# Pooled attention and a gated channel mix on one core: the product with v in groups of 128, 128, 128, 128 and 64 queries

## The chip, the cores and the metric

The kernel runs on one core of a Trainium2 chip. Such a core has five engines that run side by side, each through its own list of instructions in a fixed order: TensorE (PE, matrix products; PEld is its loading of weights), VectorE (DVE), ScalarE (ACT), GpSimd (POOL) and SyncE (SP, which here issues all DMAs). They wait for each other through semaphores. The metric is the time on the device in microseconds (us), the median of the timed runs.

## The reference

Inputs are q, k and v of 8 images x 8 heads x 1152 positions x 64, and the weights of the channel mix. What is computed, cut to what matters:

```python
q_pool = q.reshape(B, H, S // 2, 2, D).mean(axis=3)          # 576 queries for each head
scores = (1 / sqrt(D)) * q_pool @ k.transpose(0, 1, 3, 2)    # 576 x 1152
attn = exp(scores - scores.max(-1))
attn = attn / (attn.sum(-1) + 1e-9)
x = (attn @ v), heads side by side                           # 8 x 576 x 512
x_prev = x moved by one position, zeros first
xk = mu_k * x + (1 - mu_k) * x_prev                          # xr the same with mu_r
k = relu(xk @ w_k) ** 2                                      # 576 x 1024
out = sigmoid(xr @ w_r) * (k @ w_v)                          # 576 x 512
```

All inputs are float32. The kernel keeps their precision with pairs of 16-bit numbers: each operand is a high part and a low part, and a product is three products (high by high, high by low, low by high).

## The kernel before

**Attention.** The 64 pairs of image and head (heads, from here on) follow each other. A head's 576 queries are 6 blocks of 96, its 1152 keys 9 chunks of 128. For each block, PE multiplies the 9 chunks of keys with the block's queries into one of three PSUM tiles `s` (L473), DVE takes the maximum over the chunks (L480), PE turns it (L483), DVE takes it over the keys (L486), PE brings it back (L488), ACT writes the bound into a spare row of the queries' low part (L491), PE adds the remaining products (L497), and ACT takes the exponential (L503). The exponentials go as 32-bit numbers into `pf`, whose last axis is the 576 queries of a head. The upper 16 bits of each are read in place as a 16-bit number: the high part. POOL turns the lower 16 bits into a tile of their own, `pl` (L505): the low part.

**The product with v.** It is made by `window`. Its groups are 128 queries wide, since the exponentials are the weights that PE loads and PE takes 128 columns. 576 is four and a half times 128, and before the change five groups start at queries 0, 128, 256, 352 and 448 (`WIN`), so that groups 3, 4 and 5 overlap by 32 queries each time. For every group PE does, for each of the 9 chunks, two products with the high part (with v's high part and a column of ones, 65 wide, L523; with v's low part, 64 wide, L525) and one with the low part (65 wide, L530): 27 products, 135 for a head. All five groups add up side by side in one PSUM tile, `a`, which is there once. When the last group is done, DVE adds a guard to the sums (L545), inverts them (L547) and multiplies (L548) into `xb`. After every second head PE turns `xb` through the same tile `a` (L560), and ACT copies it into `xt`, in two pieces of 384 and 192 queries (L563).

**The channel mix.** Its rows are taken 256 at a time over the images. ACT and DVE make xk and xr (L632, L635), ACT and POOL their parts (L641, L643), and PE makes the three products (all on L663) into PSUM tile `f`. Rows of an image can be mixed when the last two heads of this image are in `xt`. The float32 weights are turned into pairs during the first heads: 20 pieces, each with one DMA, three steps on DVE (L594, L595, L597), two on ACT (L592, L599) and one on POOL (L600).

**What sets the order.** The kernel doesn't issue an operation where it is written. `op` records each piece with its engine, an assumed duration, the names that it reads and writes, and a key (a due time); `Issue.run` then plays the whole program with these durations and an assumed delay between engines, tries some orders, and writes the best one out. So each engine's list is fixed when the program is built, and one changed operation can move others everywhere. A group's key is that of the block after which it can begin (`after` in the last lines of the loop over heads).

Of the kernel before, what the change touches and what calls it, by code (L numbers as in the profile page):

```python
# [29 lines left out]
SQ = 0.25  # L30
# [3 lines left out]
SHIFT = 18.0  # L34
LO, VLO = 2.0 ** -28, 2.0 ** -12
# [223 lines left out]
def kernel(  # L259
# [20 lines left out]
    QN = 96  # L280
# [1 line left out]
    T = 256  # L282

    WIN = [(0, 1), (128, 2), (256, 3), (352, 4), (448, 5)]
    NW = len(WIN)
    TURN = [(0, 3, 0), (3, 5, 384)]
    assert D == 64 and DM == NG * P and TQ == NB * QN == WIN[-1][0] + P

    const = ctx.enter_context(tc.tile_pool(name="const", bufs=1))  # L290
    psum = ctx.enter_context(tc.tile_pool(name="psum", bufs=1, space=PSUM))
# [13 lines left out]
    def half(x, dt, t):  # L305

        return x.bitcast(dt).rearrange("p c (q t) -> p c q t", t=2)[:, :, :, t]
# [18 lines left out]
    NV = 3  # L326
    vt = bufs("vt", NV, [P, NC, 2 * D + 2], F16)
    vb = bufs("vb", NV, [P, NC, D + 2], F16)
    pf = const.tile([P, NC, TQ], I32, name="pf")
    pl = const.tile([P, NC, TQ], F16, name="pl")  # L330
    mx, mb = bufs("mx", 3, [P, QN], F16), bufs("mb", 3, [P, 1], F16)
    den, xb = bufs("den", 2, [P, NW], F32), bufs("xb", 1, [P, NW, 2, D], F32)
# [120 lines left out]
    def block(n, j, i, t):  # L453

        hp, z = n % 2, i % 3
        qi = n // 2 % 2
        q0 = hp * TQ + j * QN
        qhi, qlo = (qT[qi][:, r].rearrange("p j x -> p (j x)")[:, q0:q0 + QN] for r in (0, 1))
        kh, kl = ([(t_, qi, hp, j, j0) for j0, j1 in ((0, 5), (5, NQ)) if q0 < j1 * P and q0 + QN > j0 * P]
                  for t_ in ("qT", "qTl"))  # L460
        s = s_b[z]
        rows = slice(j * QN, (j + 1) * QN)
        mxz, mbz = mx[z], mb[z]

        def cols(c0, c1):
            return s[:, P + c0 * QN:P + c1 * QN]

        def grid(c0, c1):
            return cols(c0, c1).rearrange("p (c q) -> p c q", q=QN)

        def scores(c0, c1):
            for c in range(c0, c1):
                nc.tensor.matmul(cols(c, c + 1), ks1[hp][:, c, :], qhi,  # L473
                                 start=(c == c0), stop=False, skip_group_check=True)
# [5 lines left out]
        op("DVE", 0.967, lambda: nc.vector.tensor_reduce(mxz, grid(0, NC).rearrange("p c q -> p q c"),  # L480
                                                         axis=AX.X, op=ALU.max),
           r=[("s", z)], w=[("mx", z)], key=t)
        op("PE", 0.054, lambda: nc.tensor.matmul(s[0:QN, 0:P], mxz, identb, start=False, stop=False,  # L483
                                                 skip_group_check=True),
           r=[("mx", z)], w=[("s", z)], key=t + O_MAX)
        op("DVE", 0.199, lambda: nc.vector.tensor_reduce(mbz[0:QN], s[0:QN, 0:P], axis=AX.X, op=ALU.max),  # L486
           r=[("s", z)], w=[("mb", z)], key=t + O_MAX)
        op("PE", 0.05, lambda: nc.tensor.matmul(s[:, 0:QN], mbz[0:QN].broadcast_to([QN, P]),  # L488
                                                 negi[0:QN, 0:QN], start=False, stop=False, skip_group_check=True),
           r=[("mb", z)], w=[("s", z)], key=t + O_MAX)  # L490
# [12 lines left out]
        op("ACT", NC * QN / 1200 + 0.051, lambda: nc.scalar.activation(  # L503
            pf[:, :, rows], grid(0, NC), AF.Exp, bias=SHIFT, scale=0.125 / (2.0 * SQ)), r=[("s", z)], w=[("pf", j)], key=t + O_EXP)
        op("POOL", NC * QN / 1000 + 0.066, lambda: nc.gpsimd.tensor_scalar(  # L505
            pl[:, :, rows], half(pf, U16, 0)[:, :, rows], LO, 1.0, op0=ALU.mult, op1=ALU.mult),
           r=[("pf", j)], w=[("pl", j)], key=t + O_REST)

    def window(n, w, t):

        b, h = divmod(n, H)
        g, hh = divmod(h, 2)
        r0 = WIN[w][0]
        jv = n % NV
        VN = D + 1
        vk = [(x, jv, c0) for x in ("vt", "vtl") for c0 in (0, 5)]
        js = range(r0 // QN, (r0 + P - 1) // QN + 1)
        a0, rows = w * VN, slice(r0, r0 + P)

        def hi(c0, c1):
            for c in range(c0, c1):
                nc.tensor.matmul(a_b[:, a0:a0 + VN], half(pf, F16, 1)[:, c, rows], vt[jv][:, c, D:D + VN],  # L523
                                 start=(w == 0 and c == 0), stop=False, skip_group_check=True)
                nc.tensor.matmul(a_b[:, a0:a0 + D], half(pf, F16, 1)[:, c, rows], vt[jv][:, c, 0:D],  # L525
                                 start=False, stop=False, skip_group_check=True)

        def lo(c0, c1):
            for c in range(c0, c1):
                nc.tensor.matmul(a_b[:, a0:a0 + VN], pl[:, c, rows], vb[jv][:, c, 0:VN],  # L530
                                 start=False, stop=(c == NC - 1), skip_group_check=True)

        for c0 in (0, 3, 6):
            op("PE", 3 * 0.0595, lambda c0=c0: hi(c0, c0 + 3),
               r=vk + [("pf", j) for j in js] + ([("a",)] if c0 or w else []), w=[("a",)], key=t)
# [9 lines left out]
        op("DVE", 0.075, lambda: nc.vector.tensor_scalar(dz, u[:, :, D], GUARD, None, op0=ALU.add),  # L545
           r=[("a",)], w=[("den", z)], key=t + O_EVAC)
        op("DVE", 0.08, lambda: nc.vector.reciprocal(dz, dz), r=[("den", z)], w=[("den", z)], key=t + O_EVAC)  # L547
        op("DVE", 0.07 + NW * D / 960, lambda: nc.vector.tensor_tensor(  # L548
            xz[:, :, hh], u[:, :, 0:D], dz.unsqueeze(2).broadcast_to([P, NW, D]), op=ALU.mult),
           r=[("den", z), ("a",)], w=[("xb", hh)], key=t + O_EVAC)  # L550
        if hh == 0:
            return
        for k0, k1, q0 in TURN:
            base = WIN[k0][0]
            qe = WIN[k1 - 1][0] + P

            def turned(k0=k0, k1=k1, base=base):
                for k_ in range(k0, k1):
                    r_ = WIN[k_][0] - base
                    nc.tensor.transpose(a_b[:, r_:r_ + P], xz[:, k_].rearrange("p h d -> p (h d)"), ident)  # L560

            op("PE", 0.11 * (k1 - k0), turned, r=[("xb", 0), ("xb", 1)], w=[("a",)], key=t + O_TURN)
            op("ACT", 0.051 + (qe - q0) / 1200, lambda q0=q0, qe=qe, base=base: nc.scalar.copy(  # L563
                xt[b % 3][:, g, 1 + q0:1 + qe], a_b[:, q0 - base:qe - base]),
               r=[("a",)], w=[("xt", b % 3, g, k0)], key=t + O_TURN)
# [52 lines left out]
    def mix(w, t0, t1, key, dk):  # L618
# [4 lines left out]
        for c in range(NG):  # L623
            t = t0
            while t < t1:
# [4 lines left out]
                xk = [("xt", b % 3, c, k0) for k0, k1, q0 in TURN  # L630
                      if q0 < s0 + ln and WIN[k1 - 1][0] + P > s0 - 1]
# [112 lines left out]
    for n in range(B * H):  # L744
# [5 lines left out]
        for j in range(NB):  # L750
            i = n * NB + j
            block(n, j, i, i * PER)
            for w, (_, after) in enumerate(WIN):
                if after == j:
                    window(n, w, i * PER + O_AV)
        if h == H - 1:
# [42 lines left out]
```

## Time and profile before

| | us |
|---|---|
| median of three runs | 1169.64 |
| the three runs | 1169.64, 1169.77, 1166.29 |
| span of the profiled execution, first to last instruction | 1166.8 |
| PE busy | 1116.0 (96%) |
| PE's weight loads busy | 928.6 (80%) |
| ACT busy | 858.8 (74%) |
| DVE busy | 834.0 (71%) |
| POOL busy | 713.1 (61%) |

The profiled execution has no time of its own beside its span. The span stands 0.5 above the fastest of the three runs and 2.8 below their median, so the runs differ among themselves by more than what lies around the span. A share of busy time is an average: the stretch in which the weights are turned (up to about 150 us), the long middle, and the end in which only the channel mix is left have different limits.

### The profile page before, as it was taken

Reading aid. Unit: us, or ns where it says so; the run is one execution under the profiler, and the core shown is the slowest. Engines: PE = TensorE matmul, PEld = TensorE weight load, DVE = VectorE, ACT = ScalarE, POOL = GpSimd, SP = SyncE. Lnnn points to the kernel's source line nnn. Section 1 sums busy time; section 2 is a strip of 40 time slices with the busy share of each in tenths; the row PEclk is TensorE's granted clock in tenths of the full one; section 3 lists DMA queues with packets and bytes.
Section 4 is the critical chain, followed back from the end, with each engine's and each line's share of the span. In section 5 each row is a group of like instructions: output and inputs, shape, how many; then the busy total and the mean of one; then the engine's idle time right before and its main releaser. Section 6 shows DMA issues by size and latency. Waiting matters only on the chain.

```text
span 1166.8 us, 45860 instructions
## 1 busy us (share of the span) xinstructions
PE 1116.0 (96%) x19504; PEld 928.6 (80%) x19504; DVE 834.0 (71%) x1558; ACT 858.8 (74%) x1746; POOL 713.1 (61%) x819
## 2 busy tenths in 40 slices
PE   3878899999999999999999999999999999999998
PEld 3767787988788887978788888979797988888565
DVE  6899987777777867777676867776677877673320
ACT  4878887887877787777777686868777778765643
POOL 3777776656666575746666575756665666543431
PEclk9899999999999999999999999999999999999999
DMA  9696845566455534555344535444544344310000
GB/s 223 180 240 171 188 101 129 120 142 113 88 116 117 136 68 103 123 113 123 87 113 114 105 89 119 113 102 108 113 114 107 93 102 93 72 27 12 19 19 28
DMA packets 222380, 126.69 MB, mean 109 GB/s; under 512 B 157664, under 2 KB 194528, under 8 KB 222176
## 3 DMA queue, kind: packets, MB, share of 16 engines
q1 hardware_dynamic: 222176, 123.77, 47.1%
q8 instruction: 152, 2.49, 0.9%
q14 instruction: 52, 0.43, 0.1%
HBM read 67.11 MB, written 9.44 MB: 66 GB/s over the span
## 4 chain that ended last, share of the span: by engine, by line
PE 84%; ACT 5%; DVE 5%; DMA 3%; issue 2%; SPq 0%; ACTq 0%; DVEq 0%
PE f L663 33%; PE s L497 11%; PE s L473 11%; PE a L530 7%; PE a L523 6%; PE a L525 6%; PE s L663 4%; ACT pf L503 2%; DVE mx L480 2%; PE s L483 2%; PE a L663 2%; PE s L488 1%; PE a L560 1%; DMA qT<-qn 1%; DMA st<-in_moe_w_r_dram 1%
## 5 line engine op out<-in xcount | busy, mean ns | idle before, releaser
L505 POOL TENSOR_SCALAR pl<-pf 128x864 f16<-128x864 uint16 x384 | 365.8, 953 | 252.0 <-ACT pf L503 221.2
L480 DVE TENSOR_REDUCE mx<-s 128x96 f16<-128x864 f32 x384 | 402.3, 1054 | 139.1 <-PE s L473 82.1
L503 ACT ACTIVATE pf<-s 128x864 int32<-128x864 f32 x384 | 338.6, 891 | 87.9 <-PE s L497 66.8
L473 PE MATMUL s<-qT,ks 128*128 128x96 f16 x3456 | 217.9, 207 | 23.6 <-DMA qT<-qn 12.0
L525 PE MATMUL a<-vt,pf 128*128 128x64 f16 x2880 | 237.6, 193 | 0.0
L523 PE MATMUL a<-vt,pf 128*128 128x65 f16 x2880 | 237.2, 193 | 0.2
L497 PE MATMUL s<-qT,ks 128*128 128x96 f16 x3456 | 216.0, 207 | 9.7 <-ACT qT L491 8.8
L473 PEld LDWEIGHTS <-ks 128*128 128x128 f16 x3456 | 183.2, 99 | 45.1 <-issue 18.2
L523 PEld LDWEIGHTS <-pf 128*128 128x128 f16 x2880 | 202.3, 98 | 5.6
L497 PEld LDWEIGHTS <-ks 128*128 128x128 f16 x3456 | 181.2, 98 | 31.2 <-issue 12.1
L525 PEld LDWEIGHTS <-pf 128*128 128x128 f16 x2880 | 193.1, 98 | 7.4 <-issue 0.4
L491 ACT ACTIVATE qT<-s 1x96 f16<-1x96 f32 x384 | 92.9, 243 | 111.2 <-PE s L488 97.5
L486 DVE TENSOR_REDUCE mb<-s 96x1 f16<-96x128 f32 x384 | 109.0, 285 | 82.0 <-PE s L483 72.4
L530 PE MATMUL a<-vb,pl 128*128 128x65 f16 x2880 | 152.7, 194 | 1.0 <-POOL pl L505 0.9
L663 PE MATMUL f<-xhk,wk_hi 128*128 128x256 f16 x496 | 135.1, 272 | 0.4 <-ACT r L690 0.4
L663 PE MATMUL f<-xhk,wk_lo 128*128 128x256 f16 x496 | 135.1, 272 | 0.0
L663 PE MATMUL f<-xlk,wk_hi 128*128 128x256 f16 x496 | 135.1, 272 | 0.0
L530 PEld LDWEIGHTS <-pl 128*128 128x128 f16 x2880 | 121.4, 98 | 6.3 <-POOL pl L505 1.6
L663 PEld LDWEIGHTS <-wk_hi 128*128 128x128 f16 x1152 | 106.2, 98 | 10.9 <-issue 0.6
L429 POOL TENSOR_TENSOR kn<-kr,kn 128x320 f16<-128x320 f32 x126 | 99.7, 802 | 20.5 <-ACT kn L424 16.1
L694 POOL TENSOR_TENSOR gl<-g 128x512 f16<-128x512 f32 x72 | 77.8, 1080 | 50.0 <-ACT g L692 47.8
L663 PE MATMUL f<-wv_hi,g 128*128 128x512 f16 x240 | 90.9, 379 | 0.9 <-ACT em L713 0.6
(93 smaller groups left out, 1989.9 us busy)
## 6 DMA issues: line engine op xcount, KB each, us to landing
kr<-in_k_dram SPq DMA_DIRECT2D x64, 288.0 KB, 3.0
vr<-in_v_dram SPq DMA_DIRECT2D x64, 288.0 KB, 3.0
qr<-in_q_dram SPq DMA_DIRECT2D x32, 320.0 KB, 3.5
ks<-ks SPq DMA_DIRECT2D x64, 144.0 KB, 2.6
out_dram<-em SPq DMA_DIRECT2D x36, 256.0 KB, 2.1
qr<-in_q_dram SPq DMA_DIRECT2D x32, 256.0 KB, 3.5
st<-in_moe_w_k_dram SPq DMA_DIRECT2D x8, 512.0 KB, 4.5
st<-in_moe_w_v_dram SPq DMA_DIRECT2D x8, 512.0 KB, 4.0
```

What stands on the lines that cost most here:

```text
L429: lambda cs=cs, en=nc.vector if ve else nc.gpsimd: en.tensor_tensor(kn[i][:, cs, D:P], kr[i][:, cs], kn[i][:, cs, 0:D], op=ALU.subtract),
L473: nc.tensor.matmul(cols(c, c + 1), ks1[hp][:, c, :], qhi, start=(c == c0), stop=False, skip_group_check=True)
L480: op("DVE", 0.967, lambda: nc.vector.tensor_reduce(mxz, grid(0, NC).rearrange("p c q -> p q c"), axis=AX.X, op=ALU.max), r=[("s", z)], w=[ ...
L486: op("DVE", 0.199, lambda: nc.vector.tensor_reduce(mbz[0:QN], s[0:QN, 0:P], axis=AX.X, op=ALU.max), r=[("s", z)], w=[("mb", z)], key=t + O ...
L491: op("ACT", 0.133, lambda: nc.scalar.activation(qlo[QN:QN + 1], s[QN:QN + 1, 0:QN], AF.Prelu, scale=1.0 - EPS, alpha=(1.0 + EPS) / (1.0 - ...
L497: nc.tensor.matmul(cols(c, c + 1), ks2[hp][:, c, :], qlo, start=False, stop=True, skip_group_check=True)
L503: op("ACT", NC * QN / 1200 + 0.051, lambda: nc.scalar.activation(pf[:, :, rows], grid(0, NC), AF.Exp, bias=SHIFT, scale=0.125 / (2.0 * SQ) ...
L505: op("POOL", NC * QN / 1000 + 0.066, lambda: nc.gpsimd.tensor_scalar(pl[:, :, rows], half(pf, U16, 0)[:, :, rows], LO, 1.0, op0=ALU.mult, ...
L523: nc.tensor.matmul(a_b[:, a0:a0 + VN], half(pf, F16, 1)[:, c, rows], vt[jv][:, c, D:D + VN], start=(w == 0 and c == 0), stop=False, skip_g ...
L525: nc.tensor.matmul(a_b[:, a0:a0 + D], half(pf, F16, 1)[:, c, rows], vt[jv][:, c, 0:D], start=False, stop=False, skip_group_check=True)
L530: nc.tensor.matmul(a_b[:, a0:a0 + VN], pl[:, c, rows], vb[jv][:, c, 0:VN], start=False, stop=(c == NC - 1), skip_group_check=True)
L663: nc.tensor.matmul(ps, terms[i][0], terms[i][1], start=(first and i == 0), stop=(i == last), skip_group_check=True)
```

## The change

Five groups stay, but the first one now has 64 queries and the others 128 without overlap: they start at 0, 64, 192, 320 and 448. The short group would leave 64 of PE's columns empty. They carry its own low parts: `pf` gets 64 more places in front (`HALF`), POOL writes the low parts of the first 64 queries there, next to their high parts, and one set of 18 products makes both halves. The nine products with the low part fall away for this group. Its rows 0 to 63 in `a` are then the products of the low parts and rows 64 to 127 those of the high ones. Two new steps for each head bring them together before the sums are inverted: ACT scales the 64 rows of low products into a small tile, `cross`, on the other 64 partitions, and DVE adds that to `a`. POOL's step for the first block is split in two (64 queries into `pf`, 32 into `pl`). The copies into `xt` are 320 and 256 wide in place of 384 and 192.

```diff
-    WIN = [(0, 1), (128, 2), (256, 3), (352, 4), (448, 5)]
+    HALF = P // 2
+    WIN = [(0, HALF, 0), (HALF, P, 1), (HALF + P, P, 3), (HALF + 2 * P, P, 4), (HALF + 3 * P, P, 5)]
-    TURN = [(0, 3, 0), (3, 5, 384)]
+    TURN = [(0, 3), (3, 5)]
...
-    pf = const.tile([P, NC, TQ], I32, name="pf")
+    pf = const.tile([P, NC, HALF + TQ], I32, name="pf")
+    cross = const.tile([P, D + 1], F32, name="cross")
...
+        def lows(to, r0, r1, buf):
+            op("POOL", NC * (r1 - r0) / 1000 + 0.066, lambda: nc.gpsimd.tensor_scalar(
+                to, half(pf, U16, 0)[:, :, HALF + r0:HALF + r1], LO, 1.0, op0=ALU.mult, op1=ALU.mult),
+               r=[("pf", j)], w=[buf], key=t + O_REST)
+        r0 = rows.start
+        if j == 0:
+            lows(half(pf, F16, 1)[:, :, 0:HALF], 0, HALF, ("pside",))
+            r0 = HALF
+        lows(pl[:, :, r0:rows.stop], r0, rows.stop, ("pl", j))
...
+        side = size < P
+        his = slice(0, P) if side else slice(HALF + r0, HALF + r0 + P)
...
-        for c0, c1 in ((0, 5), (5, NC)):
+        for c0, c1 in () if side else ((0, 5), (5, NC)):
             op("PE", (c1 - c0) * 0.030, lambda c0=c0, c1=c1: lo(c0, c1),
...
+        up = slice(HALF, P)
+        op("ACT", 0.25, lambda: nc.scalar.activation(cross[up], a_b[0:HALF, 0:VN], AF.Copy, scale=VLO),
+           r=[("a",)], w=[("cross",)], key=t + O_EVAC)
+        op("DVE", 0.16, lambda: nc.vector.tensor_tensor(a_b[up, 0:VN], a_b[up, 0:VN], cross[up], op=ALU.add),
+           r=[("cross",), ("a",)], w=[("a",)], key=t + O_EVAC)
```

Three places of the lists of instructions show what moved. The first is on PE, in the 21st head, where its first group ends (line numbers of the changed program are 6 to 21 higher; `vt` and `vb` hold v's parts, a number behind a name is that of a buffer). Before:

```order
L523 LDWEIGHTS pf
L523 MATMUL a<-vt_87,pf 128x65
L525 LDWEIGHTS pf
L525 MATMUL a<-vt_87,pf 128x64
L530 LDWEIGHTS pl
L530 MATMUL a<-vb_90,pl 128x65
```

The last pair of products with the high part is followed by the nine with the low part, of which the first stands here. In the changed program the short group and the second one stand behind each other, and this is where their products with the high part end:

```order
L538 LDWEIGHTS pf
L538 MATMUL a<-vt_87,pf 128x65
L540 LDWEIGHTS pf
L540 MATMUL a<-vt_87,pf 128x64
L494 LDWEIGHTS mb_97
L494 MATMUL s_129<-negi,mb_97 128x96
L684 LDWEIGHTS wk_lo
L684 MATMUL f<-xhk,wk_lo 128x256
```

What follows is work of the scores (`s`) and of the channel mix (`f`); the only products with `pl` left are the second group's own, further down. Over the whole program PE has 2304 products with `pl` in place of 2880, and all its other products as before.

The second place is on DVE, at the end of the 8th head, where the weights are still being turned (L594, L595, L597 before). Before:

```order
L595 SCALAR_TENSOR_TENSOR f<-st_120,f 128x512
L480 TENSOR_REDUCE mx_95<-s_130 128x96
L545 TENSOR_SCALAR den_100<-a 128x5
L597 SCALAR_TENSOR_TENSOR ex_116<-st_120,f 128x512
L443 SCALAR_TENSOR_TENSOR vt_87<-vr_72,vt_87 128x5x64
L486 TENSOR_REDUCE mb_98<-s_130 96x1
L547 RECIPROCAL den_100<-den_100 128x5
```

After:

```order
L486 TENSOR_REDUCE mx_96<-s_131 128x96
L492 TENSOR_REDUCE mb_98<-s_130 96x1
L564 TENSOR_TENSOR a<-a,cross 64x65
L566 TENSOR_SCALAR den_101<-a 128x5
L568 RECIPROCAL den_101<-den_101 128x5
L492 TENSOR_REDUCE mb_99<-s_131 96x1
L569 TENSOR_TENSOR xb_102<-a,den_101 128x5x64
```

The new addition (L564) stands ahead of the three steps that empty `a`, and a maximum of the next block (L492) behind it; the steps of the weights that stood among them are elsewhere.

The third place is on ACT, at the end of the same head. The new step that the addition waits for is `cross` (L562):

```order
L620 CAST wv_hi<-ex_117 128x512
L430 CAST kn_77<-kr_71 128x4x64
L562 ACTIVATE cross<-a 64x65
L497 ACTIVATE qT_83<-s_129 1x96
L613 ACTIVATE f<-st_122 128x512
```

Before, the end of that head had no step on ACT until `a` was copied into `xt`; this is ACT's list there:

```order
L491 ACTIVATE qT_84<-s_129 1x96
L491 ACTIVATE qT_84<-s_130 1x96
L599 CAST wv_hi<-ex_117 128x512
L563 COPY xt_102<-a 128x384
L503 ACTIVATE pf<-s_129 128x9x96
```

What moved: `cross` now stands between the conversions (L620, L430) and the bound of a block (L497) that PE waits for.

More of the change, by code (lines that the diff above doesn't have):

```diff
@@ L282, with spans @@
     T = 256
-    WIN = [(0, 1), (128, 2), (256, 3), (352, 4), (448, 5)]
+    HALF = P // 2
+    WIN = [(0, HALF, 0), (HALF, P, 1), (HALF + P, P, 3), (HALF + 2 * P, P, 4), (HALF + 3 * P, P, 5)]
     NW = len(WIN)
-    TURN = [(0, 3, 0), (3, 5, 384)]
+    TURN = [(0, 3), (3, 5)]
     assert D == 64 and DM == NG * P and TQ == NB * QN == WIN[-1][0] + P
+    def spans(k0, k1):
+        return WIN[k0][0], WIN[k1 - 1][0] + WIN[k1 - 1][1]
     const = ctx.enter_context(tc.tile_pool(name="const", bufs=1))
@@ L503, in block @@
         op("ACT", NC * QN / 1200 + 0.051, lambda: nc.scalar.activation(
[L504 to L507, printed above, removed]
+            pf[:, :, HALF + rows.start:HALF + rows.stop], grid(0, NC), AF.Exp, bias=SHIFT, scale=0.125 / (2.0 * SQ)), r=[("s", z)], w=[("pf", j)], key=t + O_EXP)
+        def lows(to, r0, r1, buf):
[7 more added lines that the diff above has]
+        lows(pl[:, :, r0:rows.stop], r0, rows.stop, ("pl", j))
     def window(n, w, t):
@@ L513, in window @@
         g, hh = divmod(h, 2)
-        r0 = WIN[w][0]
+        r0, size, _ = WIN[w]
+        side = size < P
         jv = n % NV
@@ L517, in window @@
         vk = [(x, jv, c0) for x in ("vt", "vtl") for c0 in (0, 5)]
-        js = range(r0 // QN, (r0 + P - 1) // QN + 1)
+        js = range(r0 // QN, (r0 + size - 1) // QN + 1)
         a0, rows = w * VN, slice(r0, r0 + P)
+        his = slice(0, P) if side else slice(HALF + r0, HALF + r0 + P)
         def hi(c0, c1):
             for c in range(c0, c1):
-                nc.tensor.matmul(a_b[:, a0:a0 + VN], half(pf, F16, 1)[:, c, rows], vt[jv][:, c, D:D + VN],
+                nc.tensor.matmul(a_b[:, a0:a0 + VN], half(pf, F16, 1)[:, c, his], vt[jv][:, c, D:D + VN],
                                  start=(w == 0 and c == 0), stop=False, skip_group_check=True)
-                nc.tensor.matmul(a_b[:, a0:a0 + D], half(pf, F16, 1)[:, c, rows], vt[jv][:, c, 0:D],
-                                 start=False, stop=False, skip_group_check=True)
+                nc.tensor.matmul(a_b[:, a0:a0 + D], half(pf, F16, 1)[:, c, his], vt[jv][:, c, 0:D],
+                                 start=False, stop=(side and c == NC - 1), skip_group_check=True)
         def lo(c0, c1):
@@ L534, in window @@
             op("PE", 3 * 0.0595, lambda c0=c0: hi(c0, c0 + 3),
-               r=vk + [("pf", j) for j in js] + ([("a",)] if c0 or w else []), w=[("a",)], key=t)
-        for c0, c1 in ((0, 5), (5, NC)):
+               r=vk + [("pf", j) for j in js] + ([("pside",)] if side else []) + ([("a",)] if c0 or w else []),
+               w=[("a",)], key=t)
+        for c0, c1 in () if side else ((0, 5), (5, NC)):
             op("PE", (c1 - c0) * 0.030, lambda c0=c0, c1=c1: lo(c0, c1),
@@ L552, in window @@
             return
-        for k0, k1, q0 in TURN:
-            base = WIN[k0][0]
-            qe = WIN[k1 - 1][0] + P
+        for k0, k1 in TURN:
+            q0, qe = spans(k0, k1)
+            base = qe - (k1 - k0) * P
             def turned(k0=k0, k1=k1, base=base):
                 for k_ in range(k0, k1):
-                    r_ = WIN[k_][0] - base
+                    r_ = WIN[k_][0] + WIN[k_][1] - P - base
                     nc.tensor.transpose(a_b[:, r_:r_ + P], xz[:, k_].rearrange("p h d -> p (h d)"), ident)
@@ L629, in mix @@
                 z = turn("tmp")
-                xk = [("xt", b % 3, c, k0) for k0, k1, q0 in TURN
-                      if q0 < s0 + ln and WIN[k1 - 1][0] + P > s0 - 1]
+                xk = [("xt", b % 3, c, k0) for k0, k1 in TURN
+                      if spans(k0, k1)[0] < s0 + ln and spans(k0, k1)[1] > s0 - 1]
                 op("ACT", ln / 1200 + 0.187, lambda x=x, s0=s0, ln=ln, z=z, c=c: nc.scalar.activation(
@@ L752 @@
             block(n, j, i, i * PER)
-            for w, (_, after) in enumerate(WIN):
+            for w, (_, _, after) in enumerate(WIN):
                 if after == j:
```

## The prediction

> **What bounds the kernel now.** I read the engines' totals first, then the same totals by stretches of time, then what PE waits for in each stretch.
>
> ```profile
> PE 1116.0 (96%) x19504; PEld 928.6 (80%) x19504; DVE 834.0 (71%) x1558; ACT 858.8 (74%) x1746; POOL 713.1 (61%) x819
> ```
>
> ```profile
> core 0: us, PE busy (x) PEld busy (x) DVE busy (x) ACT busy (x) POOL busy (x), PEclk, DMA share, GB/s
> 40.00:140.00 100.00, 80.32 (x1793) 71.27 (x1794) 97.40 (x185) 81.73 (x164) 75.10 (x83) 1.00 0.82 192
> 160.00:1080.00 920.00, 913.86 (x16531) 770.71 (x16532) 673.19 (x1256) 699.60 (x1430) 578.11 (x660) 1.00 0.47 103
> 1080.00:1160.00 80.00, 80.00 (x510) 49.72 (x509) 18.79 (x36) 40.72 (x81) 26.36 (x32) 1.00 0.05 21
> ```
>
> The total of 96% hides two regimes. From 40 to 140 us, while the weights are turned, DVE is busy for 97.40 of 100 us and PE for 80.32: DVE paces. From 160 us on PE is busy for 913.86 of 920 us and the others for 73% to 76% (DVE, ACT) and 63% (POOL); in the last 80 us PE never rests. The granted clock is 1.00 in all three rows, so it plays no part in what follows.
>
> What PE waits for, by the waits of the same two stretches (line waited for, total us, times, longest), the first fence from 40 to 140 us, the second from 160 to 1080 us:
>
> ```profile
> PE s L473 <- ACT pf L503: 7.7, 18, 1.0
> PE s L488 <- DVE mb L486: 5.3, 9, 1.8
> ```
>
> ```profile
> PE s L473 <- ACT pf L503: 2.0, 5, 0.7
> ...
> PE a L560 <- ACT xt L563: 0.5, 1, 0.5
> ```
>
> In the middle there is next to nothing to win by shorter waits (PE is idle for 920 - 913.86 = 6.1 us in all), and only 0.5 us belong to tile `a`, which the change holds longer. What counts there is how much PE has to do. Where one regime gives way to the other is told by the first product of the channel mix, and by how many heads have been emptied by then:
>
> ```profile
> L663 PE MATMUL f<-xhk,wk_hi x32: 269/272/273, 152.3 to 167.1; 128*128 128x256 f16 x32
> ```
>
> ```profile
> L545 DVE TENSOR_SCALAR den<-a x9: 144/153/166, 39.7 to 152.5; 128x5 f32<-128x5 f32 x9
> ```
>
> ```profile
> L530 PE MATMUL a<-vb,pl x2475: 191/193/198, 163.6 to 1075.3; 128*128 128x65 f16 x191
> ```
>
> At 152.3 us the mix begins and PE has work in stock from then on. Nine heads are through by 152.5 us; the 2475 products with `pl` after 160 us are 55 x 45, so exactly 55 heads do their products with v in the stretch that PE paces.
>
> **The change, part by part.**
>
> *The nine products that go.* The duration that a row gives for one matmul (0.19 us) is its way through the array; the price is the step to the next. Timeline of PE, start, duration, count:
>
> ```profile
> 703.08 0.45 PE L530 MATMUL a<-vb,pl 128*128 128x65 f16 x9
> 703.36 0.19 PE L523 MATMUL a<-vt,pf 128*128 128x65 f16 x1
> ...
> 703.91 0.45 PE L530 MATMUL a<-vb,pl 128*128 128x65 f16 x9
> 704.19 0.38 PE L663 MATMUL f<-wr_hi,xr 128*128 128x512 f16 x1
> ```
>
> Nine take 0.28 us both times (703.36 - 703.08, 704.19 - 703.91), 31 ns each. In the 55 heads that PE paces this is 55 x 0.28 = 15.4 us off the end. In the first nine heads it is another 2.5 us, which I count at nothing, since PE waits there anyway. If both counted it would be 17.9.
>
> The Trainium skill, "TensorE: Matmul & The Clock Gate", section "Back-to-back issue gap", gives N/2.4 + 2.5 ns for a lone matmul, which for 65 columns is 29.6 ns and would make the term 14.7 us, and about 81 ns at N = 128 for a stream of pairs of weight load and product, with which it would be 40. The trace lies near the first, with 31 ns in just such a stream, and I go by the trace.
>
> *The two steps that come.* Neither exists in the trace. Neighbours by shape, the second number behind the first bar is the mean ns of one:
>
> ```profile
> L548 DVE TENSOR_TENSOR xb<-a,den 128x320 f32<-128x320 f32 x64 | 31.1, 486 | 1.3
> ...
> L563 ACT COPY xt<-a 128x384 f32<-128x384 f32 x32 | 15.4, 482 | 9.5 <-PE a L560 9.2
> ...
> L563 ACT COPY xt<-a 128x192 f32<-128x192 f32 x32 | 10.2, 320 | 0.6
> L545 DVE TENSOR_SCALAR den<-a 128x5 f32<-128x5 f32 x64 | 10.1, 158 | 13.3 <-PE a L530 12.0 <-PE s L488 0.6
> ```
>
> DVE's addition has 65 elements; between 158 ns for 5 and 486 for 320 the line gives 0.22 us. These two rows are its bounds. ACT's step, by the line through 320 ns for 192 and 482 for 384, is 0.21 us; zero and 0.32 bound it. In the middle both lie on engines with a quarter of their time free. Between 40 and 140 us DVE has nothing free, so there the addition counts in full: of the nine early heads the first ends before 40 us, eight remain, 8 x 0.22 = 1.8 us (1.3 to 3.9 by the bounds). Behind the addition on DVE's list stand the steps that empty `a` and the maxima (L480, L486) that PE waits for. If the addition comes to the head of the list before `cross` is done, all of them stand still. A late `cross` costs at most what ACT has ahead of it; by the order that is a conversion, so I allow 0.5 us for each of the eight heads, 4 us, and take nothing, since the row of L545 from 0 to 155 us names no idle time before it.
>
> *The longer hold on `a`.* End of one head in the middle, PE and DVE out of the timeline:
>
> ```profile
> 711.53 0.45 PE L530 MATMUL a<-vb,pl 128*128 128x65 f16 x9
> ...
> 712.44 0.49 DVE L548 TENSOR_TENSOR xb<-a,den 128x320 f32<-128x320 f32 x1
> ...
> 715.32 0.49 PE L560 MATMUL a<-ident,xb 128*128 128x128 f32 x3
> ```
>
> DVE is done with `a` at 712.93; PE comes back to it at 715.32, having done mix and scores in between. The new steps lengthen this by 0.21 + 0.22 us and one more change of engine, an estimate of 0.55 together, against 2.4 us of room. So nothing, with the mix as cover. If that cover were gone, each head would pay up to 0.55 us.
>
> *POOL's split.* Again two rows by shape:
>
> ```profile
> L505 POOL TENSOR_SCALAR pl<-pf 128x864 f16<-128x864 uint16 x384 | 365.8, 953 | 252.0 <-ACT pf L503 221.2 <-PE a L530 7.1 <-PE s L483 3.7
> ...
> L446 POOL TENSOR_SCALAR vb<-vr 128x576 f16<-128x576 f32 x64 | 43.9, 686 | 56.4 <-PE a L530 38.8 <-DMA vr<-in_v_dram 5.5 <-DMA qr<-in_q_dram 4.4
> ```
>
> The rows of 864 and 576 elements give 0.93 ns for an element and 0.15 us for an instruction. One more instruction for each head is 64 x 0.15 = 9.8 us on an engine that has 453 us free: nothing. With places of four bytes between its outputs the first part might be slower; twice its 0.69 us would still be 44 us in free time. The two copies into `xt` keep their 576 elements, and no DMA changes.
>
> POOL's rows do touch DVE's, though, as these two from 104 us show beside DVE's mean for the same shape:
>
> ```profile
> 104.10 1.08 POOL L505 TENSOR_SCALAR pl<-pf 128x864 f16<-128x864 uint16 x1 [1.20 <-ACT pf L503]
> ```
>
> ```profile
> 104.49 1.03 DVE L443 SCALAR_TENSOR_TENSOR vt<-vr,vt 128x320 f16<-128x320 f32 x1
> ```
>
> ```profile
> L443 DVE SCALAR_TENSOR_TENSOR vt<-vr,vt 128x320 f16<-128x320 f32 x64 | 37.0, 578 | 0.0
> ```
>
> Beside a POOL step DVE's took 1.03 us in place of 0.58. By the Trainium skill, "SBUF — State Buffer", section "Who interferes with whom", a DVE instruction with two SBUF inputs and a GpSimd instruction that reads SBUF shut each other out for a whole instruction. The trace agrees in that row. By that rule eight early heads could lose another 8 x 0.15 = 1.2 us on DVE, and the time would be 1157.2. I don't count it, since most of DVE's steps there read PSUM, and keep it for the range.
>
> *The order.* All lists are written anew. Ahead of the first product of the mix, the list of PE holds the scores of one block less than before, and DVE's list, ahead of the mix's fourth step (L635), one maximum and one piece of the weights more. DVE from 40 to 140 us, by shape:
>
> ```profile
> L480 DVE TENSOR_REDUCE mx<-s 128x96 f16<-128x864 f32 x42 | 43.5, 1047 | 1.8 <-PE s L488 0.6 <-PE s L473 0.6 <-issue 0.2
> ...
> L595 DVE SCALAR_TENSOR_TENSOR f<-st,f 128x512 int32<-128x512 int32 x16 | 10.9, 681 | 0.0
> ```
>
> The lesser work on PE speaks for an earlier start, a maximum of 1.05 us and three steps of some 0.68 on DVE for one up to 3.1 us later. I take nothing for the two together.
>
> *The sum.* Against the span: 1166.8 - 15.4 + 1.8 = 1153.2. The median of the runs lies 2.84 above the span of the profiled execution, and I carry this over: **1156.0 us**.
>
> **The rivals.**
>
> *The early stretch costs more.* DVE waits for `cross` (4 us), the start of the mix slips by the moved steps (3.1 us): 1163.1. For it speaks that DVE is at 97% there and any wait is added to the end; against it, that DVE idles before none of its steps on `a` there.
>
> *The gain doesn't reach the end.* PE's free time stays free, because the other engines pace the middle: 1169.6 + 1.8 = 1171.4. Against it: the middle leaves 24% to 37% of each of them, and PE is idle there for 6.1 us. For it: the lists are fixed, so that PE meets a late partner wherever the assumed durations are too short. That the products aren't removed at all is out: the list holds 576 fewer.
>
> *Slower: `a` becomes the bound.* The place is the end of a head, where PE stands before the next head's first product, or before L560, with `a` still in DVE's and ACT's hands. At 0.55 us for each of 64 heads against 0.28 saved, the time is 1169.6 + 64 x 0.27 = 1187. It decides from a wait of 0.28 us a head. Against it stand the 2.4 us of room and the single wait of 0.5 us.
>
> *More than the middle's share.* The early 2.5 us count too, and shorter lists of PE end some waits: 1166.8 - 17.9 + 2.84 = 1151.7, and down to 1150 with part of the 6.1 us of idle time gone.
>
> **How the numbers follow.** Forecast (1152 to 1160): 0.66. Early stretch costs more (1160 to 1166): 0.13. More than the middle's share (below 1152): 0.08. No gain at the end (1166 to 1173): 0.07. Slower by `a`: 0.06. A measurement of this kernel can tell about 0.3% from no change, that is 1166.1 to 1173.2. So faster is 0.66 + 0.13 + 0.08 = 0.87, no change 0.07, slower 0.06. The range takes in the forecast, the rival above it up to 1164 (one of the two slips in full, the other in part) and the one below down to 1150.
>
> **What would show it.** In the changed profile: PE's products with `pl` 2304 in place of 2880; from 160 us to the last head PE still busy for over 99%, with that stretch about 15 us shorter; no wait of PE on `cross`'s addition or on `a` of more than 1 us in all; the first product of the mix at 152 to 156 us; the addition near 0.22 us; DVE at 97% from 40 to 140 us. The prediction is wrong if the mix begins after 158 us, if PE is idle in the middle for more than 12 us, or if the steps of the remaining products with `pf` become longer than 30 ns.

## The result and the profile after

| | before | after |
|---|---|---|
| median, us | 1169.7 (1166.29 to 1170.91, 4 runs) | 1159.8 (1158.5 to 1162.38, 4 runs) |
| ratio to before, 95% interval | | 0.9919 [0.9904, 0.9933] |
| span of the profiled execution, us | 1166.8 | 1156.7 |
| first product of the mix, us | 152.3 | 157.1 |
| from there to the end, us | 1014.5 | 999.6 |

The changed kernel is 9.9 us faster; 13.6 were predicted. Read first the engines' totals of the changed kernel, then two stretches of it (columns as in the prediction: us, then the busy time of PE, PEld, DVE, ACT and POOL, then the granted clock, DMA share, GB/s).

```profile
PE 1105.0 (96%) x18928; PEld 916.0 (79%) x18928; DVE 859.4 (74%) x1622; ACT 875.9 (76%) x1810; POOL 740.0 (64%) x883
```

```profile
40.00:140.00 100.00, 79.53 (x1632) 71.11 (x1632) 92.19 (x178) 78.76 (x161) 72.92 (x84) 0.91 0.72 180
160.00:1080.00 920.00, 915.14 (x16209) 766.79 (x16207) 707.20 (x1331) 724.59 (x1507) 610.59 (x726) 1.00 0.47 103
```

PE has 576 products less, as announced, and the middle is as full as before. The early stretch isn't: DVE falls from 97.40 to 92.19, PE doesn't gain by it, and the granted clock, 1.00 in the row of before, is 0.91. The start of the mix and the two new steps:

```profile
L684 PE MATMUL f<-xhk,wk_hi x32: 269/272/273, 157.1 to 178.3; 128*128 128x256 f16 x32
```

```profile
L562 ACT ACTIVATE cross<-a x64: 217/218/220, 39.9 to 1065.4; 64x65 f32<-64x65 f32 x64
L564 DVE TENSOR_TENSOR a<-a,cross x64: 243/244/244, 40.9 to 1065.6; 64x65 f32<-64x65 f32 x64
```

The steps last 0.218 and 0.244 us, against estimates of 0.21 and 0.22. The mix starts 4.8 us later where 1.8 was expected; what follows is 14.9 us shorter, against 15.4. That looks like one right and one mis-sized term. The experiments show that the 14.9 hides a cost and a gain that the prediction didn't have.

PE's waits from 160 to 1070 us in the changed kernel (line waited for, total us, times, longest):

```profile
PE s L494 <- DVE mb L492: 1.1, 3, 0.5
PE f L684 <- ACT em L734: 1.0, 3, 0.5
PE s L479 <- ACT pf L509: 0.9, 2, 0.7
PE a L538 <- ACT xt L584: 0.4, 1, 0.4
```

A wait on `a` appears once, for 0.4 us: the longer hold is hidden, as the prediction had it.

**The clock.** The halved clock is found by cutting the early stretch finer. Before, then changed kernel, from 40 to 50 and from 80 to 90 us:

```profile
40.00:50.00 10.00, 8.49 (x211) 7.89 (x212) 9.84 (x19) 8.05 (x17) 7.66 (x9) 1.00 0.75 170
80.00:90.00 10.00, 8.16 (x161) 6.74 (x157) 9.79 (x20) 8.55 (x17) 7.37 (x8) 1.00 0.95 200
```

```profile
40.00:50.00 10.00, 7.24 (x97) 6.39 (x97) 9.17 (x17) 6.98 (x15) 7.49 (x10) 0.66 0.67 186
80.00:90.00 10.00, 7.05 (x95) 6.35 (x92) 8.51 (x19) 6.73 (x16) 6.89 (x8) 0.70 0.76 213
```

And around one such place, PE's timeline and the windows of the changed kernel:

```profile
81.88 0.26 PE L489 MATMUL s<-identb,mx 128*96 128x128 f16 x1 [0.36 <-DVE mx L486]
84.11 0.64 PE L503 MATMUL s<-qT,ks 128*128 128x96 f16 x6 [1.97 <-ACT qT L497]
```

```profile
77.30:80.70 3.40, 2.75 (x68) 2.46 (x65) 3.40 (x7) 3.05 (x5) 1.52 (x2) 1.00 0.55 142
80.70:84.10 3.40, 1.07 (x26) 0.90 (x23) 3.13 (x6) 0.96 (x5) 2.82 (x4) 0.99 0.87 238
84.10:91.00 6.90, 6.28 (x67) 5.75 (x67) 5.68 (x13) 6.07 (x12) 4.30 (x5) 0.51 0.55 164
91.00:95.00 4.00, 3.09 (x91) 2.96 (x88) 4.00 (x10) 3.58 (x8) 1.74 (x4) 1.00 1.00 125
```

PE waits 1.97 us for one bound, has been busy for 1.07 of 3.40 us, and then works 6.9 us at half its clock. With the places at 43 and 132 us the changed kernel has 17.1 us of it between 40 and 140 us. The profiled execution of the kernel before has none there, but that isn't so in all of its executions: the profile of its repeat (under other lists, below) has two pieces of 3.4 us, at 70 and at 80 us.

### The profile page after: what moved, and what is told of

It is laid out like the page before. It is cut to its first block, busy times and chain, and to the rows that moved or that the text cites. A ratio compares the mean times of both kernels' runs of the same rounds, so it can differ in the third digit from the quotient of the medians.

```text
span 1156.7 us, 44885 instructions
## 1 busy us (share of the span) xinstructions
PE 1105.0 (96%) x18928; PEld 916.0 (79%) x18928; DVE 859.4 (74%) x1622; ACT 875.9 (76%) x1810; POOL 740.0 (64%) x883
## 4 chain that ended last, share of the span: by engine, by line
PE 85%; DVE 5%; ACT 4%; DMA 3%; issue 2%; SPq 1%; ACTq 0%; DVEq 0%
PE f L684 33%; PE s L479 11%; PE s L503 11%; PE a L538 7%; PE a L540 7%; PE a L545 6%; PE s L684 4%; ACT pf L509 2%; DVE mx L486 2%; PE s L489 2%; PE a L684 2%; PE s L494 1%; PE a L581 1%; DMA ks<-kn 1%; DMA kr<-in_k_dram 1%
## 5 line engine op out<-in xcount | busy, mean ns | idle before, releaser
L512 POOL TENSOR_SCALAR pl<-pf 128x864 f16<-128x864 uint16 (+1 forms) x384 | 337.8, 880 | 186.3 <-ACT pf L509 157.9
L538 PE MATMUL a<-vt,pf 128*128 128x65 f16 x2880 | 230.2, 194 | 1.5 <-ACT pf L509 0.9
L540 PE MATMUL a<-vt,pf 128*128 128x64 f16 x2880 | 230.4, 194 | 0.0
L492 DVE TENSOR_REDUCE mb<-s 96x1 f16<-96x128 f32 x384 | 109.3, 285 | 79.9 <-PE s L489 71.8
L497 ACT ACTIVATE qT<-s 1x96 f16<-1x96 f32 x384 | 92.1, 242 | 88.4 <-PE s L494 75.7
L545 PE MATMUL a<-vb,pl 128*128 128x65 f16 x2304 | 124.0, 194 | 0.2 <-POOL pl L512 0.2
L545 PEld LDWEIGHTS <-pl 128*128 128x128 f16 x2304 | 99.2, 98 | 5.1 <-POOL pl L512 0.5
L489 PE MATMUL s<-identb,mx 128*96 128x128 f16 x384 | 87.6, 228 | 6.8 <-DVE mx L486 6.7
```

Of the source, the lines that this page charges most:

```text
L512: op("POOL", NC * (r1 - r0) / 1000 + 0.066, lambda: nc.gpsimd.tensor_scalar(to, half(pf, U16, 0)[:, :, HALF + r0:HALF + r1], LO, 1.0, op0= ...
L540: nc.tensor.matmul(a_b[:, a0:a0 + D], half(pf, F16, 1)[:, c, his], vt[jv][:, c, 0:D], start=False, stop=(side and c == NC - 1), skip_group ...
```

## The experiments

Four causes were open: the removed products are worth less than 15.4; the two new steps cost more than 1.8; the halved clock costs time; the rewritten lists are better or worse by themselves. An edit below that leaves an operation out leaves its place in the order as it was. All ratios are to the kernel before, each against runs on the same chip.

**The removed products alone.** In the kernel before, the nine products of the first group with the low part are left out (so the low parts of its queries are missing), in every head, or from the tenth head on:

```diff
         def lo(c0, c1):
             for c in range(c0, c1):
+                if w == 0 and n >= 0:      # the other kernel: n >= 9
+                    return
```

> The kernel before with the first group's nine products with the low part left out for every head (that part of the result is left out too), and nothing else: every engine's list stands as before, the nine products are only missing. Theory 1 (the granted clock: with less to do PE falls below the share that keeps its clock full while DVE paces, and the clock halves there): the stretch from 160 us on gets about 15 us shorter, but the clock shows new halved intervals between 40 and 150 us and the mix begins 2 to 4 us later than 152.3; about 1156 to 1157 us, ratio 0.989. Theory 2 (the new steps on ACT and DVE cost the early stretch): no new step here, so the mix begins at 152 us and the time is 1169.7 - 15.4 = 1154.3, ratio 0.987. Theory 3 (the rewritten order costs the early stretch): as theory 2.

> The same, but the nine products are left out only from the tenth head on, so that PE has the same work as before while DVE paces. Theory 1: clock as before (one halved interval near 26 us), the mix begins at 152 us, and the time is 1169.7 - 15.4 = 1154.3, 2 to 3 us less than the run that leaves them out everywhere. Theories 2 and 3: the same 1154.3, and no difference from the other run.

Measured: 1156.3 us, 0.9884 [0.9869, 0.9900], in every head; 1155.83, 0.9878 [0.9863, 0.9893], from the tenth on. That is 13.6 and 14.3 us (1.16% and 1.22% of 1169.7); the predicted 15.4 lies just beyond the end of the first interval (15.3) and inside the second (16.0). The two kernels don't differ by more than the noise, so the first nine heads' products are worth nothing that could be measured, as counted. The mix starts here at

```profile
L665 PE MATMUL f<-xhk,wk_hi x32: 269/272/273, 150.7 to 165.3; 128*128 128x256 f16 x32
```

(every head left out), so with the old lists nothing is late. Less work on PE in the early stretch is thus not by itself what halves the clock: in this profile it stays at 1.00 from 40 to 140 us.

**The two steps left out.** In the changed kernel `cross` and the addition are left out, in all heads or in the first nine (the short group's low parts then stay apart):

```diff
-        op("ACT", 0.25, lambda: nc.scalar.activation(cross[up], ...
+        op("ACT", 0.25, lambda: None,      # the other: n >= 9 and nc.scalar.activation(...
-        op("DVE", 0.16, lambda: nc.vector.tensor_tensor(a_b[up, 0:VN], ...
+        op("DVE", 0.16, lambda: None,      # the other: n >= 9 and nc.vector.tensor_tensor(...
```

> The changed kernel without the two new steps (ACT's cross and DVE's addition are left out for every head, and with them the low parts of the first 64 queries); all other rows of the lists keep their order. Theory 1: PE has as little to do as in the changed kernel, so the clock halves between 40 and 150 us here too; DVE saves 8 x 0.24 = 1.9 us there, the mix begins at 155 us, 1157.5 us. Theory 2: the whole early loss goes, the mix begins at 152 to 153, 1155 us. Theory 3: only the 1.9 us go, and the clock has no part in it: 1158.

> The changed kernel without ACT's cross and DVE's addition in the first nine heads (their low parts of the first 64 queries are left out there), with both from the tenth head on; all other rows keep their order. If the two steps cost their time while DVE paces, this run is as fast as the one without them anywhere (ratio 0.9855) and the mix begins at 154.8. If they cost it in the stretch that PE paces, the ratio is that of the changed kernel, 0.992. By the trace I expect about half and half: the mix at 154.8, ratio 0.9885.

Measured: 1153.15, 0.9855 [0.9842, 0.9869], without them; 1156.15, 0.9888 [0.9871, 0.9905], with them from the tenth head on. So they cost about 7 us in all (0.9919 - 0.9855, or 0.9912 - 0.9855 by the repeat of the changed kernel below). How this divides is less sure. Some 3.9 us (0.9888 - 0.9855, intervals that barely part) come with the steps of the middle, where the prediction had put nothing; 3.6 us, or 2.8 by the repeat, come with the first nine heads, but there the intervals overlap. The start of the mix, without them and with them from the tenth head on:

```profile
L683 PE MATMUL f<-xhk,wk_hi x32: 269/272/274, 154.8 to 176.0; 128*128 128x256 f16 x32
```

```profile
L684 PE MATMUL f<-xhk,wk_hi x32: 269/273/274, 154.7 to 175.9; 128*128 128x256 f16 x32
```

The changed kernel's start at 157.1 is 2.4 us later, which is the delay by the early steps; 8 x 0.244 is 2.0.

The two kernels have the same lists on PE, so their traces can be laid over each other product by product from there on. The one with the steps falls 4.1 us behind; 3.7 of it arise at ten places of 0.2 us or more, eight of them PE waiting for a maximum (L489, L494). One of them, without the steps (DVE, then POOL):

```profile
505.60 0.48 DVE L400 SCALAR_TENSOR_TENSOR qn<-qs,qn 128x320 f16<-128x320 f32 x1
506.00 0.18 DVE L567 RECIPROCAL den<-den 128x5 f32<-128x5 f32 x1
506.22 0.29 DVE L491 TENSOR_REDUCE mb<-s 96x1 f16<-96x128 f32 x1
```

```profile
505.73 1.13 POOL L511 TENSOR_SCALAR pl<-pf 128x864 f16<-128x864 uint16 x1 [0.81 <-ACT pf L508]
```

and with them (DVE, POOL, PE):

```profile
506.48 0.24 DVE L564 TENSOR_TENSOR a<-a,cross 64x65 f32<-64x65 f32 x1
...
507.29 1.23 DVE L401 SCALAR_TENSOR_TENSOR qn<-qs,qn 128x320 f16<-128x320 f32 x1
508.44 0.18 DVE L568 RECIPROCAL den<-den 128x5 f32<-128x5 f32 x1
508.54 0.24 DVE L492 TENSOR_REDUCE mb<-s 96x1 f16<-96x128 f32 x1
```

```profile
507.27 0.91 POOL L512 TENSOR_SCALAR pl<-pf 128x864 f16<-128x864 uint16 x1 [1.19 <-ACT pf L509]
```

```profile
508.84 0.22 PE L494 MATMUL s<-negi,mb 96*128 96x96 f16 x1 [0.25 <-DVE mb L492]
```

Without the addition DVE's `qn` starts 0.13 us ahead of POOL's `pl`, takes 0.48 us, and POOL's step is the long one. The addition puts `qn` 0.02 us behind POOL, and now `qn` takes 1.23 us, the maximum behind it is late, and PE stands. At four of the ten places, 1.9 of the 3.7 us, a DVE step on two SBUF tiles has grown like this. The Trainium skill, "SBUF — State Buffer", section "Who interferes with whom", says that the order of issue decides who is blocked; these rows agree. The start of a row isn't exact to 0.1 us: at one of the four the DVE row starts 0.04 us ahead of POOL's, but the row before it on DVE ends 0.05 us behind POOL's start. The other places have only the shift itself.

How much such places cost hangs on the moment. The changed kernel has the same lists and steps from the tenth head on and begins its mix 2.4 us later, but its trace, laid over that of the kernel with the late steps alone, ends only 0.4 us later: six of the ten places, 2.0 us together, aren't there. By the traces the steps of the middle thus cost 4.1 us in the one kernel and 2.1 us in the other, and the early steps between 0.4 and 2.3 us. The two parts don't simply add. Together they are 4.4 us by the traces and about 7 by the times, since the profiled execution without the steps is the slowest of its four and that of the changed kernel the fastest of its four.

**The addition without its wait.** DVE waits 11.8 us for `cross` in the changed kernel, 13 times. Here `cross` is made in the first nine heads only, and the later additions read the ninth head's values (so the short group's own low parts are left out from there on):

```diff
-        op("ACT", 0.25, lambda: nc.scalar.activation(cross[up], ...
+        op("ACT", 0.25, lambda: n < 9 and nc.scalar.activation(cross[up], ...
```

> The changed kernel without the copy to cross from the tenth head on; the addition stays and reads the ninth head's values, so the short group's low halves are wrong from there. Theory that DVE's wait for ACT's copy (11.8 us, 13 times) makes the maxima late for PE in the middle: nearly the 3.6 us of both steps come back, 1156.3. Rival, that the addition's own 0.24 us does it: less than 1 us comes back, 1159.

Measured: 1159.76, 0.9916 [0.9899, 0.9932]: nothing comes back that could be measured. In its trace the steps of the middle stand as follows:

```profile
L564 DVE TENSOR_TENSOR a<-a,cross x64: 243/244/244, 41.3 to 1066.7; 64x65 f32<-64x65 f32 x64
L562 ACT ACTIVATE cross<-a x9: 218/218/220, 40.3 to 166.8; 64x65 f32<-64x65 f32 x9
```

The middle of this trace, product by product, is 0.9 us shorter than that of the changed kernel, and still 1.2 us longer than that of the kernel without the steps. So DVE's 11.8 us of waiting cost at most 0.9 us, and what is left is the addition's own place on DVE. Each of these figures is the difference of two single traces.

**The clock.** First, 45 products of 65 columns for each of the first nine heads, into unused columns of `a`:

```diff
         def hi(c0, c1):
             for c in range(c0, c1):
+                if n < WARM:      # WARM = 9
+                    nc.tensor.matmul(a_b[:, NW * VN:NW * VN + VN], half(pf, F16, 1)[:, c, his], ...
```

> The changed kernel with 45 additional products of 65 columns for each of the first nine heads, into columns of tile a that nobody reads, inside the pieces that are there already, so that all lists keep their order. Theory 1: PE's clock keeps full over most of 40 to 150 us, the mix begins at 153 to 155 us in place of 157.1, and although PE does 12 us more the time falls to about 1156 to 1157. Theory 2: nothing on DVE or ACT changes; the mix begins at 157 and the time stays near 1159.8 or above it. Theory 3: as theory 2.

Measured: 1165.44, 0.9959 [0.9946, 0.9972], some 5 us slower than the changed kernel, and the granted clock from 40 to 140 us still 0.95. Products put where PE is busy lengthen its list and don't fill its gaps, so this didn't test the clock. Second, products of 32 columns only behind lines 489 and 494, and only where the changed kernel's trace has PE waiting over 0.2 us there, to 0.8 of each wait; third, the same in the kernel before, in its own gaps:

```diff
+    WARM = {'mx': {8: 21, 9: 28, 10: 27, ...}, 'mb': {8: 11, 9: 18, ...}}   # 746 products; before: 598
+    def warm(what, s):
+        ...
+        for _ in range(WARM[what].get(k, 0)):
+            nc.tensor.matmul(s[:, P + NC * QN:1024], identb, identb[:, 0:1024 - P - NC * QN], ...
```

> The changed kernel with 746 additional products of 32 columns in all, put behind L489 and L494 in the first nine heads only where the changed kernel's trace shows PE waiting for more than 0.2 us, as many as fill 0.8 of that wait, into columns of s that nobody reads; all lists keep their order. Theory 1 (the clock that halves in the early stretch costs time there): fewer halved intervals between 36 and 150 us, and the mix begins 2 to 4 us earlier than 157.1; about 1157 us. Theory 2 (the two new steps cost the early stretch) and theory 3 (the rewritten order does): the mix begins at 157 us or later, 1159.8 or more.

> The kernel before with 598 products of 32 columns into unused columns, behind the products of lines 483 and 488 where its own trace has PE waiting over 0.2 us in the first nine heads (0.8 of each wait), as was done to the changed kernel. Clock theory: the kernel before has a halved clock only from 26 to 36 us, ahead of these products, so there is nothing to win: 1169 to 1171.5. Rival, that such products help by something else than the clock (a busy array, shorter waits behind them): the 3.4 us that the changed kernel won, 1166.5.

Measured: in the changed kernel 1156.29, 0.9886 [0.9871, 0.9900]; in the kernel before 1170.98, 1.0018 [1.0005, 1.0031]. Their early stretches, the changed one first:

```profile
40.00:140.00 100.00, 89.15 (x2286) 82.23 (x2283) 93.86 (x180) 80.52 (x163) 75.32 (x86) 1.00 0.76 182
```

```profile
40.00:140.00 100.00, 90.13 (x2284) 83.28 (x2280) 95.78 (x176) 80.05 (x160) 73.39 (x80) 1.00 0.76 190
```

With 746 products more, the changed kernel's clock stays at 1.00 and it is 3.4 us faster than its own repeat beside it (1159.66, next paragraph; the intervals, [0.9871, 0.9900] and [0.9897, 0.9928], just overlap); the mix starts here at

```profile
L695 PE MATMUL f<-xhk,wk_hi x32: 270/272/273, 154.2 to 175.4; 128*128 128x256 f16 x32
```

The kernel before, whose two profiles have 0 and 6.8 us of it there, wins nothing and loses 1 to 2 us. So such products don't help as such. That speaks for the clock as the cause in the changed kernel; the last kernel below sets a limit to it.

The times on record say more, since each execution has its mean clock beside it. Executions of one kernel have the same lists and still differ in clock: 0.991 to 0.997 for the kernel before. Over the 124 executions whose clock is on record, each set against the mean of its own kernel on its chip, 0.001 less of clock goes with 0.74 us more (standard error 0.06). As 0.001 of 1160 us is 2.3 us at half the clock, that is some 0.3 us for each us halved, and 5 us for the 17.1 us above. It isn't proof of a cause, since an execution whose waits are longer for another reason would show both. The products themselves cost something too: at a clock of 0.996 or 0.997 the kernel before took 1168.1 us without them and 1170.4 with them (medians of seven each).

**Other lists.** New random draws for the planner's trials (`11 + i` for `1 + i`), in the changed kernel and in the one before, were to give other lists:

> The changed kernel with other random draws where the orders are compared, so the same work in another order. Theory 3 (which order comes out decides a few us): the mix begins somewhere between 151 and 160 us, and the time differs from 1159.8 by 2 to 4 us. Theories 1 and 2: the mix begins at 156 to 158 us and the time stays within 2 us.

> The kernel before with the same other draws. Theory 3: the time differs from 1170 by 2 to 4 us, so that part of what the change seems to give or cost is luck of the order. Theories 1 and 2: within 2 us of 1170, the mix begins at 151 to 153 us.

They left the lists of all four computing engines as they were, so these two are repeats and tell nothing of the lists: 1159.66, 0.9912 [0.9897, 0.9928], and 1170.42, 1.0001 [0.9992, 1.0011]. What does give other lists is the measured duration of the new steps in the planner:

```diff
-        op("ACT", 0.25, lambda: nc.scalar.activation(cross[up], ...
+        op("ACT", 0.22, lambda: nc.scalar.activation(cross[up], ...
-        op("DVE", 0.16, lambda: nc.vector.tensor_tensor(a_b[up, 0:VN], ...
+        op("DVE", 0.25, lambda: nc.vector.tensor_tensor(a_b[up, 0:VN], ...
```

> The changed kernel with 0.22 and 0.25 us as the planner's durations of the two new steps in place of 0.25 and 0.16 (measured 0.218 and 0.244), so that the lists are written anew. Theory that in the middle PE meets late maxima because the planner takes the addition for 0.16 us: the lists leave room for it and 2 to 3 us come back, 1157. Rival, that the places where PE waits are an accident of each list: any time from 1156 to 1163, told apart by the number of PE's waits for maxima after 160 us (some dozen now) staying as it is. Clock theory: whatever the lists, the start of the mix is late by the length of the halved stretches between 40 and 140 us (17 us now) times 0.2.

Measured: 1157.25, 0.9897 [0.9879, 0.9916], against 0.9912 for the repeat and 0.9919 for the first measurement, with intervals that overlap: some 2 us better, if anything. The mix starts late, at

```profile
L684 PE MATMUL f<-xhk,wk_hi x32: 270/272/273, 161.3 to 178.4; 128*128 128x256 f16 x32
```

and the rest is short: 1154.9 - 161.3 = 993.6 us. After 160 us PE waits for a maximum once, 0.3 us, where the changed kernel has three waits and 1.1 us, which was the sign named for the planner's wrong duration as a cause. The early clock is worse (first row; 23.9 us are halved, not the 20.4 of the next expectation), so the last kernel fills its gaps in the same way, with 723 products (second row):

> The changed kernel with the measured durations in the planner (as in retimed) and 723 products of 32 columns into unused columns, behind the products of lines 489 and 494 where the trace of retimed has PE waiting over 0.2 us in the first nine heads (0.8 of each wait). Clock theory: the halved stretches between 40 and 140 us (20.4 us in retimed) go, and with them 0.2 us for each of theirs, 4 us: 1153.3. Rival, that the 3.4 us won on the first list was particular to that list: 1157.

```profile
40.00:140.00 100.00, 80.31 (x1612) 72.24 (x1612) 91.86 (x173) 76.67 (x156) 70.30 (x82) 0.88 0.70 173
```

```profile
40.00:140.00 100.00, 87.28 (x2191) 80.64 (x2189) 93.50 (x175) 78.99 (x160) 72.92 (x84) 0.98 0.77 179
```

Measured: 1156.54, 0.9893 [0.9876, 0.9909], not to be told apart from 0.9897. The clock came back, but for one piece of 3.4 us, and the forecast of 1153.3 failed. So the 3.4 us don't carry over to any list as they are. Since each of the two gains, 3.4 and some 0.5 us, is uncertain by 2 to 3 us, the two kernels don't prove that the price differs either. Which of the three places in the changed kernel costs the 3.4 us, and whether it is the clock there or the filled gaps in some other way, wasn't separated.

The changed kernel with filled gaps (1156.29, [0.9871, 0.9900]) beats the kernel before and the first measurement of the changed one with intervals apart, though not that of its repeat. The two with the corrected durations have medians in between, and their intervals touch that of the changed kernel, [0.9904, 0.9933].

## Why the prediction came out as it did

The time, 1159.8, lies in the range and at the upper edge of the forecast's 1152 to 1160. By its steps, the measured ones from the ratios:

| step | predicted, us | measured, us |
|---|---|---|
| 55 heads without nine products | -15.4 | -13.6 and -14.3 |
| first nine heads' products | 0 | 0 (the two do not differ) |
| two new steps, first nine heads | +1.8 | +2.8 to +3.6 (intervals overlap; 0.4 to 2.3 by traces) |
| two new steps, middle | 0 | +3.9 (2.1 to 4.1 by traces) |
| rewritten lists, with POOL's split and the other copies (without the new steps, against the removed products alone) | 0, up to +3.1 | -3.4 |
| longer hold on `a`, POOL's split | 0 | no wait seen over 0.4 |

That -13.6, -3.4, +3.9 and +3.6 add up to the whole is no test, since each is the difference of two neighbours in one chain of kernels.

- **The removed products** were right, or 1 to 2 us too high: 31 ns each, in the stretch that PE paces, and nothing measurable ahead of it.
- **The new steps in the middle** are the step that failed: "both lie on engines with a quarter of their time free". DVE has that time, but not in front of the maxima that PE is about to need. 55 x 0.244 = 13.4 us of addition became 2 to 4 us of waiting. The prediction had seen POOL stretch a DVE step from 0.58 to 1.03 us, and priced this for the early heads alone.
- **The early steps** were mis-sized: the start of the mix slips by 2.4 us against 1.8, and the halved clock lies in the same stretch. "The granted clock is 1.00 in all three rows, so it plays no part" was true of that execution of the kernel before and false of the changed one. In the profiles of the six kernels with new lists and unfilled gaps the clock is halved for 17 to 24 us between 40 and 155 us; in the four with the old lists (the kernel before, its repeat, and the two with products removed) for 0 to 6.8 us. The mean clock of every execution says the same, 0.984 to 0.991 against 0.991 to 0.997. So the order brings most of it, which a row of before couldn't show.
- **The lists** gave 3.4 us where nothing was counted (0.9855 against 0.9884, intervals that touch). The mix starts 4.1 us later with them (154.8 against 150.7), more than the 3.1 that the prediction allowed for the moved steps, and the rest is shorter (1152.3 - 154.8 = 997.5 against 1152.9 - 150.7 = 1002.2), but since other work stands ahead of that product, this doesn't locate the gain. It stays open.
- **The signs.** Held: 2304 products with `pl`, PE over 99% after 160 us (915.14 of 920), idle there for 4.9 us and not 12, no wait on `a` above 1 us, the remaining products with `pf` 30.0 ns apart as before. Failed: the start of the mix, 157.1 against 152 to 156, and DVE at 92% and not 97% from 40 to 140 us.
- **Two readings** were off without consequence. 64 x 0.15 is 9.6, not 9.8. And the bound of 3.1 us for the moved steps counts three of DVE's steps on the weights; ahead of the mix's fourth step the changed list has one of them more (L618), and with the one maximum that is 1.05 + 0.68 = 1.7 us.

The errors of the lists and of the new steps in the middle nearly cancel (-3.4 and +3.9). Without the gain by the lists the time would have been some 1163 us, still in the range but outside the forecast. That it came out inside was luck to this extent, and no proof of the terms.

## What to carry to other kernels

An engine with free time is no cover by itself: look at what stands behind the new step in its list, and whether the step pushes a neighbour behind another engine's access to the same memory. What it costs hangs on the moment, here 2 or 4 us with the same lists, so one pair of traces doesn't give the price. Where a change thins out the tensor engine's work, or alters its order, in a stretch with waits, read the granted clock there in pieces of a few microseconds; the mean over the span (0.988) hides it. Filling such gaps with idle products gained 3.4 us on one list and nothing that could be measured on a second, and lost 1 to 2 us on a third, so the length of the halved time alone is no estimate of the gain. Where a planner assumes durations, give it the measured ones.

## What the runs showed of the hardware

- No long wait is needed for a halved clock. In the changed kernel it came after a wait of 1.97 us, with PE busy for 1.07 of the 3.40 us ahead of it. At the two other places the longest waits were 0.71 and 0.81 us, and the windows ahead had PE busy for more:

```profile
39.70:43.10 3.40, 1.42 (x21) 1.03 (x20) 3.23 (x6) 3.30 (x9) 3.07 (x4) 1.00 0.79 243
128.40:131.80 3.40, 1.80 (x25) 1.29 (x26) 3.28 (x9) 3.28 (x7) 2.65 (x4) 1.00 0.64 204
```

The kernel before kept its full clock after a wait of 1.76 us, though PE was busy for less than in the second of these rows:

```profile
76.90:80.30 3.40, 1.64 (x44) 1.50 (x41) 3.40 (x8) 2.53 (x6) 2.89 (x4) 1.00 1.18 316
80.30:83.70 3.40, 2.90 (x71) 2.54 (x67) 3.40 (x8) 2.77 (x6) 2.72 (x4) 1.00 1.15 198
```

So neither the longest wait nor the busy time orders these four windows. The columns that PE's products stream in them do: counted from the traces, some 1450, 1980 and 2430 were followed by the halved clock, and 3210 were not.

The halved stretches last 6.8, 6.8 and 3.4 us. The Trainium skill, "TensorE: Matmul & The Clock Gate", section "What's actually happening", gives a free-running window of 3413 ns, which these lengths fit; its advice to leave no idle gap of more than some 3 us (section "Why this matters for your kernels") doesn't cover this trace, where the longest gaps ahead of the three stretches were 1.97, 0.71 and 0.81 us. What counts here is the work in a window, not one gap.

- A DVE step of 0.48 us took 1.23 us when it started 0.02 us behind a POOL step, and 0.48 when it started 0.13 us ahead.
